# Cosine attention into a highway layer on one Trainium2 core: Newton steps on VectorE for the inverse norms, half of the highway tiles combined in PSUM, and a re-planned order of work

## Chip, core and metric

One core of a Trainium2 chip. The metric is the device time of one execution in microseconds (us), the median of several. Engines are named as in the profile: PE is TensorE's matmul, PEld its weight load, DVE is VectorE, ACT is ScalarE, POOL is GpSimd, SP is SyncE. SP and POOL also issue the DMAs, each in the order of its own instruction stream.

## What is computed

```
q, k, v: [8, 12, 448, 64] float32 (batch, heads, sequence, head size), tau = 0.1
q_n = q / (norm(q) + 1e-6);  k_n = k / (norm(k) + 1e-6)
attn = softmax(q_n @ k_n^T / tau);   y = attn @ v
x = y with heads side by side: [8 * 448 = 3584 tokens, 12 * 64 = 768]
H = max(x @ w_h, 0);  T = sigmoid(x @ w_t + b_t)        w_h, w_t: [768, 768]
out = T * H + (1 - T) * x                                float32
```

## The kernel before

The work is cut two ways. Attention goes by batch (8 batches b), quad (3 per batch: four heads) and pair (two per quad, 48 in all, number n). The highway layer goes by tiles of 128 tokens (28 tiles m: three per batch and, for every second batch, one that gathers the rows left over from two batches).

For each batch the steps are these. POOL issues four loads of q and k into `raw` (L290; six for batch 0), each cast from float32 to float16 on the way. SP issues three loads of v into `vraw` (L311 to L315). VectorE squares q and k (`sq`, L337), folds the squares twice (`f1`, L344; `f2`, L351) and sums them to the squared norms `n2` (`red`, L356). That happens twice per batch, once for each half. Then the inverse norms `rs` are made from `n2`. For batches 0 and 1 this is `newton` (L363 to L373, on VectorE): a shift and a subtraction on the bits for a first guess, then two rounds of three instructions. For batches 2 to 7 it is `power` (L375 to L379): one POOL instruction that raises all 84 norms of each partition to the power -0.5. POOL multiplies q and k by `rs` into `qkn`, six instructions per quad (L411 to L420). SP transposes `qkn` into `qkT` by DMA (L465, two per quad). TensorE multiplies q by k (`sc` and `sl` in PSUM, L508 and L511), ScalarE takes exp into `ex` (L522, L524), TensorE multiplies by v (32 matmuls per pair into a bank of `pb`, L545), and VectorE divides by the row sums: `rd`, `xb`, `st` (L553 to L559).

When the six pairs of a batch are done, SP copies the left-over rows (`sh`, L578) and transposes `xb` into `xT` by DMA (L596). A highway tile is then four matmul groups `ff` (L608, with a bias matmul L611 in the last two), each into one bank of `pb`. The two of w_h are read by VectorE, `d = max(h, 0) - x` (L619). The two of w_t are read by ScalarE, `t = tanh(z / 2)` (L626), into the SBUF tile `t`. Then `g` makes `t = (t + 1) / 2` (L637, VectorE or POOL), `h` makes `d = t * d` (L642, VectorE), `o` makes `o = d + x` (L650, POOL or VectorE), and SP stores `o` (L665).

PSUM has eight banks: four for `sc`, one for `sl` and three for `pb`. The ring of three `pb` banks is shared by the attention product and all four matmul groups of each highway tile.

The order of every engine's instructions is fixed ahead of time by a small planner in Python (class `Planner`). It simulates the engines with a cost in nanoseconds for each step, picks on each free engine the ready step with the lowest number `step` (plus an offset for an engine that is second choice), and writes the instructions out in that order. On the chip each engine runs its stream strictly in that order, so an instruction that waits holds up all behind it. The planner takes 2500 ns for a `power` step. It lets a load be issued while the modelled DMA queue is at most `DEPTH = 2500` ns behind, and lets every DMA land `LATE = 1900` ns after its turn. A step's `takes` and `drops` say which ring slot it takes and frees: `t` frees its `pb` bank when the tanh is done.

Of the kernel before, what the change touches and what calls it, by code (L numbers as in the profile page):

```python
# [44 lines left out]
class Planner:  # L45
# [4 lines left out]
    LATE = 1900  # L50
    DEPTH = 2500
# [112 lines left out]
def kernel(  # L164
# [162 lines left out]
    for b in range(B):  # L327
        parts = [(0, 2), (2, 4), (4, 6)] if b == 0 else [(0, 3), (3, 6)]
        reds = []
        for lo, hi in parts:  # L330
# [68 lines left out]
    for k_ in range(NQUAD):  # L399
# [322 lines left out]
```

## Time and profile before

| | us |
|---|---|
| three executions: lowest, median, highest | 388.15, 389.93, 394.87 |
| the profiled execution, device time | 391.11 |
| its span in the trace | 389.3 |
| busy in it: PE / POOL / DVE / ACT | 270.4 / 261.7 / 206.0 / 184.3 |

The profiled execution is 1.81 us longer than its span, and 1.18 us longer than the median of the three. Busy time is the time in which an engine had an instruction under way. A busy PE may still be slow, because its granted clock varies (1.00 is the upper of its two levels, 2.4 GHz; 0.50 is 1.2 GHz, and a stretch's figure is a mean). The DMA share is the mean over the core's 16 DMA engines of the time in which a packet was under way; packets overlap, so it goes above 1.

### The profile page before, as it was taken

How to read it: one execution, taken by the hardware profiler on the slowest of the kernel's cores; microseconds unless marked ns; L12 is line 12 of the kernel's file. 1: busy time of each engine (PE TensorE's matmuls, PEld its weight loads, DVE VectorE, ACT ScalarE, POOL GpSimd, SP SyncE). 2: the span in 40 equal slices, each digit the busy share in tenths (PEclk: the TensorE clock that was granted, in tenths of full speed). 3: DMA queues.
4: the chain of work that ended last, by engine and by line, in shares of the span. 5: the costliest groups of instructions: out<-in, count | busy, mean ns of one | idle time of the engine just before them, and what ended most of it. 6: DMA issues, size and time to landing. Idle time of an engine off the chain costs nothing.

```text
span 389.3 us, 6889 instructions
## 1 busy us (share of the span) xinstructions
PE 270.4 (69%) x2676; PEld 152.5 (39%) x2676; DVE 206.0 (53%) x403; ACT 184.3 (47%) x268; POOL 261.7 (67%) x225
## 2 busy tenths in 40 slices
PE   0157467991669819399371697836997996898593
PEld 0125233551215505245141364413553654454262
DVE  1899931588415245474385456706784464154133
ACT  1067456682037805537265144801874566366021
POOL 7346773339999996579984998799729992012031
PEclk9998785997569967979886698986998999699698
DMA  7993999999476299995799999944986069311724
GB/s 153 213 191 73 169 181 173 180 222 230 74 133 132 29 168 191 174 211 108 111 146 157 170 192 148 184 61 93 213 158 131 2 121 165 93 42 43 130 50 115
DMA packets 104259, 53.81 MB, mean 138 GB/s; under 512 B 74529, under 2 KB 100641, under 8 KB 104226
## 3 DMA queue, kind: packets, MB, share of 16 engines
q1 hardware_dynamic: 89794, 40.00, 57.3%
q0 software_dynamic: 14432, 13.37, 24.6%
q8 instruction: 21, 0.34, 0.4%
q14 instruction: 12, 0.10, 0.1%
HBM read 39.32 MB, written 11.01 MB: 129 GB/s over the span
## 4 chain that ended last, share of the span: by engine, by line
PE 30%; POOL 29%; DMA 15%; issue 10%; DVE 9%; SPq 4%; ACT 2%; POOLq 1%; DVEq 0%; ACTq 0%
PE pb L608 18%; POOL rs L377 14%; PE pb L545 6%; POOL qkn L420 4%; DMA qkT<-qkn 4%; PE sc L508 4%; DMA raw<-in_k_dram 4%; DMA vraw<-in_v_dram 3%; DMA xT<-xb 3%; POOL qkn L417 2%; POOL qkn L415 2%; DMA out_dram<-o 2%; DVE sq L337 2%; POOL raw L290 2%; POOL t L637 2%
## 5 line engine op out<-in xcount | busy, mean ns | idle before, releaser
L522 ACT ACTIVATE ex<-sc 128x896 f16<-128x896 f32 x144 | 126.1, 924 | 72.1 <-PE sc L508 71.8
L608 PEld LDWEIGHTS <-xT 128*128 128x128 f16 x672 | 68.2, 108 | 123.7 <-issue 52.1
L608 PE MATMUL pb<-w_h,xT 128*128 128x384 f16 x336 | 77.1, 387 | 52.3 <-DMA xT<-xb 42.3
L377 POOL TENSOR_TENSOR rs<-n,half 128x84 f32<-128x84 f32 x6 | 82.8, 13804 | 11.7 <-DVE n L356 9.2
L626 ACT ACTIVATE t<-pb 128x384 f16<-128x384 f32 x56 | 27.6, 493 | 106.1 <-PE pb L611 102.3
L608 PE MATMUL pb<-w_t,xT 128*128 128x384 f16 x336 | 70.4, 350 | 7.1 <-DVE st L559 6.6
L508 PE MATMUL sc<-qkT 64*128 64x448 f16 x288 | 51.8, 392 | 27.5 <-DMA qkT<-qkn 15.9
L545 PE MATMUL pb<-vp,ex 128*128 128x65 f16 x1536 | 62.5, 199 | 5.7 <-DVE d L619 2.0
L650 POOL TENSOR_TENSOR o<-d,xb 128x768 f32<-128x768 f16 x14 | 23.6, 1685 | 61.6 <-DVE d L642 54.7
L545 PEld LDWEIGHTS <-ex 128*128 128x128 f16 x1536 | 58.4, 102 | 16.2 <-issue 10.5
L337 DVE TENSOR_TENSOR sq<-raw 128x2688 f16<-128x2688 f16 (+1 forms) x17 | 30.1, 1771 | 40.1 <-DMA raw<-in_k_dram 40.1
L619 DVE SCALAR_TENSOR_TENSOR d<-pb,xb 128x384 f16<-128x384 f32 x48 | 26.2, 554 | 35.8 <-PE pb L608 35.7
L420 POOL TENSOR_TENSOR qkn<-raw,rs 128x384 f16<-128x384 f16 x45 | 39.9, 902 | 0.1
L637 DVE TENSOR_SCALAR t<-t 128x768 f16<-128x768 f16 x19 | 8.4, 443 | 49.0 <-ACT t L626 49.0
L508 PEld LDWEIGHTS <-qkT 64*128 64x128 f16 x288 | 12.7, 95 | 52.5 <-issue 30.2
L555 DVE TENSOR_TENSOR xb<-pb,rd 128x384 f16<-128x384 f32 x48 | 26.8, 558 | 1.8
L415 POOL TENSOR_TENSOR qkn<-raw,rs 128x448 f16<-128x448 f16 x23 | 22.6, 982 | 7.5 <-DVE rs L372 7.5
L642 DVE TENSOR_TENSOR d<-t,d 128x768 f16<-128x768 f16 x28 | 19.6, 699 | 14.8 <-POOL t L637 14.1
L524 ACT ACTIVATE ex<-sl 128x448 f16<-128x448 f32 x48 | 26.3, 549 | 0.0
L417 POOL TENSOR_TENSOR qkn<-raw,rs 128x384 f16<-128x384 f16 x22 | 24.2, 1098 | 0.0
L553 DVE RECIPROCAL rd<-pb 128x7 f32<-128x7 f32 x48 | 9.6, 199 | 27.4 <-PE pb L545 27.3
L477 POOL TENSOR_TENSOR vp<-vraw,mask 128x768 f16<-128x768 f32 x8 | 12.8, 1599 | 12.2 <-DMA vraw<-in_v_dram 8.6
(56 smaller groups left out, 231.3 us busy)
## 6 DMA issues: line engine op xcount, KB each, us to landing
out_dram<-o SPq DMA_DIRECT2D x48, 192.0 KB, 3.4
vraw<-in_v_dram SPq DMA_DIRECT2D x8, 768.0 KB, 9.7
raw<-in_q_dram POOLq DMA_DIRECT2D x14, 336.0 KB, 7.4
raw<-in_k_dram POOLq DMA_DIRECT2D x14, 336.0 KB, 6.7
vraw<-in_v_dram SPq DMA_DIRECT2D x8, 576.0 KB, 9.0
vraw<-in_v_dram SPq DMA_DIRECT2D x8, 192.0 KB, 8.5
out_dram<-o SPq DMA_DIRECT2D x4, 384.0 KB, 2.5
w_h<-in_moe_w_h_dram POOLq DMA_DIRECT2D x2, 576.0 KB, 9.2
```

What stands on the lines that cost most here:

```text
L337: nc.vector.tensor_mul(sq_r[key][:, 0:n].rearrange("p (t s) d -> p t (s d)", t=2), r, r)
L377: nc.gpsimd.tensor_tensor(out=rs_r[b][:, :, :], in0=n2_r[b][:, :, :], in1=half[:, :].unsqueeze(2).to_broadcast([128, 2, 42]), op=ALU.pow)
L415: eng.tensor_mul(qkn[:, 0:7, 0, :], raw[:, 0, 0], rs[:, 0, 0].unsqueeze(2).to_broadcast([128, 7, D]))
L417: eng.tensor_mul(qkn[:, 1:7, 1, :], raw[:, 0, 1, 0:6], rs[:, 0, 1, 0:6].unsqueeze(2).to_broadcast([128, 6, D]))
L420: eng.tensor_mul(qkn[:, 7:13, g, :].rearrange("p (j i) d -> p i j d", i=2), raw[:, 1, g, 0:6, :].rearrange("p (i j) d -> p i j d", i=2), r ...
L508: nc.tensor.matmul(sc_r[n, j][:, g, 0:S], lhsT=T[:, 448 + 128 * j : 576 + 128 * j], rhs=rhs, start=True, stop=True)
L522: nc.scalar.activation(o, sc_r[n, j][:, :, 0:S], AF.Exp, scale=inv_tau)
L524: nc.scalar.activation(ex[:, 3136 : 3136 + S], sl_r[n][:, 0:S], AF.Exp, scale=inv_tau)
L545: nc.tensor.matmul(u[:, s * 65 : s * 65 + 65], lhsT=l, rhs=r, start=(m == 0), stop=(m == len(ms) - 1))
L555: nc.vector.tensor_tensor(out=xo, in0=u[:, 0:6, 0:D].rearrange("p (g i) e -> p g i e", g=2), in1=rd[:, 0:6].rearrange("p (g i) -> p g i", ...
L608: nc.tensor.matmul(pt[:, 0:MH], lhsT=xT[:, c, :], rhs=w_sb[w][:, c, ms], start=(c == 0), stop=(w == 0 and c == CC - 1))
L626: nc.scalar.activation(t_r[m][:, h], pb_r[m, w, h][:, 0:MH], AF.Tanh, scale=0.5)
```

## The change

Four things are changed. The inverse norms of all eight batches are made by `newton` on VectorE; `power` and its constant `half` are gone. Every second highway tile (odd m, `flat`) is combined in place: tanh writes back into its PSUM bank, VectorE makes `e = (t + 1) * d` in that bank and then `o = 0.5 * e + x` into SBUF, each by halves of 384, and the bank is freed after that. In the other tiles `g` is always on VectorE. The planner treats the SBUF port that VectorE and POOL share as exclusive: a step marked `"port"` doesn't start, in the plan, while one on the other engine holds it. And loads are issued in one order over POOL and SP: a load waits, in the plan, while an earlier-numbered one is ready, and the modelled queue may be 800 ns deep instead of 2500. Several costs are set anew.

```diff
-    LATE = 1900
-    DEPTH = 2500
+    LATE = {"load": 2400, "turn": 2500, "xturn": 1900, "": 1500}
+    DEPTH = 800
...
+            first = min((o.step for q in ready.values() for t, o in q if t <= now and o.dma is not None and o.dma[1] == "load"),
+                        default=0.0)
...
-                    if op.dma is not None and op.dma[1] == "load" and dma_free > now + self.DEPTH:
+                    if op.dma is not None and op.dma[1] == "load" and (dma_free > now + self.DEPTH or op.step > first):
+                        continue
+                    if "port" in op.engs[e] and port_free > now:
                         continue
...
+                if "port" in op.engs[e]:
+                    port_free = now + dur
...
-        def power(b):
-            def fn(op):
-                nc.gpsimd.tensor_tensor(out=rs_r[b][:, :, :], in0=n2_r[b][:, :, :],
-                                        in1=half[:, :].unsqueeze(2).to_broadcast([128, 2, 42]), op=ALU.pow)
-            return fn
...
-            if b < 2:
-                o = add(f"nw{b}_{lo}", ("DVE", 8 * (195 + 14 * (hi - lo) * 1.042)), 6 * b + lo - 4.5, newton(b, lo, hi), **kw)
-            else:
-                o = add(f"nw{b}_{lo}", ("POOL", 2500), 6 * b + lo - 4.5, power(b), **kw)
-                o.deps.append(ini_m)
+            o = add(f"nw{b}_{lo}", ("DVE", 8 * (195 + 14 * (hi - lo) * 1.042), "port"), 6 * b + lo - 4.5, newton(b, lo, hi), **kw)
...
+    FLAT = lambda m: m % 2 == 1
...
-                    def t_fn(op, m=m, w=w, h=h):
-                        nc.scalar.activation(t_r[m][:, h], pb_r[m, w, h][:, 0:MH], AF.Tanh, scale=0.5)
+                    def t_fn(op, m=m, w=w, h=h, flat=flat):
+                        src = pb_r[m, w, h][:, 0:MH]
+                        nc.scalar.activation(src if flat else t_r[m][:, h], src, AF.Tanh, scale=0.5)
...
+        if flat:
+            oo = []
+            for h in range(2):
+                def e_fn(op, m=m, h=h):
+                    t = pb_r[m, 1, h][:, 0:MH]
+                    nc.vector.scalar_tensor_tensor(out=t, in0=t, scalar=1.0, in1=d_r[m][:, h], op0=ALU.add, op1=ALU.mult)
+
+                ee = add(f"e{m}_{h}", ("DVE", 590), s0 + 0.8, e_fn, deps=[el[h], el[2 + h]], drops=[(d_r, m)] if h else [])
+
+                def o_fn(op, m=m, h=h, xsrc=xsrc):
+                    ms = slice(h * MH, h * MH + MH)
+                    nc.vector.scalar_tensor_tensor(out=o_r[m][:, ms], in0=pb_r[m, 1, h][:, 0:MH], scalar=0.5,
+                                                   in1=xsrc()[:, ms], op0=ALU.mult, op1=ALU.add)
+
+                oh = add(f"o{m}_{h}", ("DVE", 590), s0 + 0.8, o_fn, deps=[ee], after=oo, takes=[] if h else [(o_r, m)],
+                         drops=[(pb_r, (m, 1, h))])
```

On POOL, around the inverse norms of batch 2 (`raw2` is its q and k, `vp` the v of the batch before, `o` a highway tile's last step). Before:

```order
L290 DMA raw0_69<-in_q_dram 128x3x448
L477 TENSOR_TENSOR vp0_91<-vraw0_89,mask_67 128x12x64
L290 DMA raw0_69<-in_k_dram 128x3x448
L377 TENSOR_TENSOR rs0_80<-n20_78,half_66 128x84
L411 TENSOR_TENSOR qkn0_83<-raw2_71,rs0_80 128x128
L413 TENSOR_TENSOR qkn0_83<-raw2_71,rs0_80 128x64
L415 TENSOR_TENSOR qkn0_83<-raw2_71,rs0_80 128x7x64
```

Of the change:

```order
L473 TENSOR_TENSOR vp0_90<-vraw0_88,mask_66 128x12x64
L296 DMA raw0_68<-in_q_dram 128x3x448
L296 DMA raw0_68<-in_k_dram 128x3x448
L407 TENSOR_TENSOR qkn0_82<-raw2_70,rs0_79 128x128
L409 TENSOR_TENSOR qkn0_82<-raw2_70,rs0_79 128x64
L411 TENSOR_TENSOR qkn0_82<-raw2_70,rs0_79 128x7x64
```

The instruction of L377 is gone from between the loads and the first multiplication of batch 2 (L411, now L407). The load of v's mask product stands where it stood.

On VectorE, in the same part of the program. Before, batch 2's second half of squares ended in the sum of L356 and nothing followed it there:

```order
L642 TENSOR_TENSOR d1_112<-t1_109,d1_112 128x768
L650 TENSOR_TENSOR o1_115<-d1_112,xb0_98 128x768
L619 SCALAR_TENSOR_TENSOR d2_113<-pb0_120,xb0_98 128x384
L619 SCALAR_TENSOR_TENSOR d2_113<-pb2_122,xb0_98 128x384
L337 TENSOR_TENSOR sq0_72<-raw2_71 128x2688
L344 TENSOR_TENSOR f10_74<-sq0_72 128x1344
L351 TENSOR_TENSOR f20_76<-f10_74 128x672
L356 TENSOR_REDUCE n20_78<-f20_76 128x2x21
L553 RECIPROCAL rd0_96<-pb1_121 128x7
```

Of the change (`e` is L639, its `o` L645, Newton L372 to L378, `red` L362):

```order
L350 TENSOR_TENSOR f10_73<-sq0_71 128x1344
L357 TENSOR_TENSOR f20_75<-f10_73 128x672
L639 SCALAR_TENSOR_TENSOR pb1_120<-pb1_120,d1_111 128x384
L645 SCALAR_TENSOR_TENSOR o1_114<-pb1_120,xb0_97 128x384
L639 SCALAR_TENSOR_TENSOR pb2_121<-pb2_121,d1_111 128x384
L645 SCALAR_TENSOR_TENSOR o1_114<-pb2_121,xb0_97 128x384
L549 RECIPROCAL rd1_96<-pb0_119 128x7
L551 TENSOR_TENSOR xb1_98<-pb0_119,rd1_96 128x2x3x64
L555 TENSOR_TENSOR st1_100<-pb0_119,rd1_96 128x64
L617 SCALAR_TENSOR_TENSOR d2_112<-pb1_120,xb0_97 128x384
L362 TENSOR_REDUCE n20_77<-f20_75 128x2x21
L617 SCALAR_TENSOR_TENSOR d2_112<-pb2_121,xb0_97 128x384
L372 TENSOR_SCALAR rs0_79<-n20_77 128x84
L373 TENSOR_SCALAR rs0_79<-rs0_79 128x84
L376 TENSOR_TENSOR nt0_81<-rs0_79 128x84
L377 SCALAR_TENSOR_TENSOR nt0_81<-nt0_81,n20_77 128x84
L378 SCALAR_TENSOR_TENSOR rs0_79<-nt0_81,rs0_79 128x84
```

Two `e` and two `o` of tile 1, which read and write the banks `pb1` and `pb2`, stand behind the folds of batch 2, and the eight Newton instructions of batch 2 (the last three are left out here) stand behind the sum and behind `d` of tile 2.

On POOL, at the start of the program. Before:

```order
L290 DMA raw0_69<-in_k_dram 128x2x448
L415 TENSOR_TENSOR qkn0_83<-raw0_69,rs0_80 128x7x64
L420 TENSOR_TENSOR qkn0_83<-raw0_69,rs0_80 128x2x3x64
L290 DMA raw1_70<-in_q_dram 128x3x448
L290 DMA raw1_70<-in_k_dram 128x3x448
L290 DMA raw1_70<-in_q_dram 128x3x448
L477 TENSOR_TENSOR vp0_91<-vraw0_89,mask_67 128x12x64
L290 DMA raw1_70<-in_k_dram 128x3x448
L270 DMA w_h_61<-in_moe_w_h_dram 128x3x768 x2
```

Of the change:

```order
L296 DMA raw0_68<-in_k_dram 128x2x448
L296 DMA raw1_69<-in_q_dram 128x3x448
L296 DMA raw1_69<-in_k_dram 128x3x448
L296 DMA raw1_69<-in_q_dram 128x3x448
L296 DMA raw1_69<-in_k_dram 128x3x448
L276 DMA w_h_61<-in_moe_w_h_dram 128x3x768
L473 TENSOR_TENSOR vp0_90<-vraw0_88,mask_66 128x12x64
L276 DMA w_h_61<-in_moe_w_h_dram 128x3x768
L407 TENSOR_TENSOR qkn2_84<-raw0_68,rs0_79 128x128
```

All four loads of batch 1 (`raw1`) and the first of the weights now stand ahead of everything on POOL that waits for data; before, two multiplications of batch 0 and the mask product of v stood between them.

The whole program has 6 `power` instructions fewer and 48 Newton instructions more; POOL has 9 of `g` and 6 of `o` fewer (15 before, 9 now); VectorE has 56 of `e` and its `o` more, 5 of `g`, 14 of `h` and 8 of `o` fewer. ScalarE does 19 of the 24 copies of v (15 before).

## Rows read from the trace of the kernel before

**Rows 1.** The page: busy time, share of the span and instructions of each engine
```profile
PE 270.4 (69%) x2676; PEld 152.5 (39%) x2676; DVE 206.0 (53%) x403; ACT 184.3 (47%) x268; POOL 261.7 (67%) x225
```

**Rows 2.** The page, part 4: shares of the chain that ended last, by engine
```profile
PE 30%; POOL 29%; DMA 15%; issue 10%; DVE 9%; SPq 4%; ACT 2%; POOLq 1%; DVEq 0%; ACTq 0%
```

**Rows 3.** The chain's pieces in order of time: start us, us, what
```profile
89.46 13.77 POOL rs L377
...
247.21 13.74 issue
```

**Rows 4.** Groups by line: busy us, mean ns of one, idle before, releaser
```profile
L377 POOL TENSOR_TENSOR rs<-n,half 128x84 f32<-128x84 f32 x6 | 82.8, 13804 | 11.7 <-DVE n L356 9.2 <-DMA qkT<-qkn 2.6
```

**Rows 5.** GpSimd in order of time, at the fifth of the chain's pieces
```profile
247.14 13.75 POOL L377 TENSOR_TENSOR rs<-n,half 128x84 f32<-128x84 f32 x1 [2.57 <-DMA qkT<-qkn]
```

**Rows 6.** Stretches: us; busy PE, PEld, DVE, ACT, POOL; clock; DMA share; GB/s
```profile
0.00:65.00 65.00, 29.44 (x317) 16.86 (x318) 40.82 (x105) 32.62 (x43) 40.57 (x60) 0.87 0.98 164
65.00:88.00 23.00, 23.00 (x238) 13.25 (x237) 16.16 (x29) 14.53 (x22) 6.82 (x7) 0.94 1.23 201
88.00:266.00 178.00, 114.15 (x1102) 62.90 (x1101) 91.77 (x152) 76.58 (x112) 156.32 (x113) 0.81 0.92 142
266.00:290.00 24.00, 23.80 (x264) 13.59 (x264) 17.09 (x31) 16.09 (x25) 15.22 (x19) 0.93 0.99 188
290.00:358.00 68.00, 60.39 (x644) 34.76 (x644) 29.72 (x68) 40.58 (x61) 36.22 (x25) 0.92 0.42 85
358.00:389.30 31.30, 19.64 (x120) 11.17 (x116) 10.44 (x22) 3.92 (x8) 6.55 (x4) 0.83 0.41 92
```

**Rows 7.** Waits of TensorE: line, releaser, us in total, times, longest
```profile
PE pb L608 <- DMA xT<-xb: 42.3, 7, 10.9
...
PE pb L608 <- DVE st L559: 16.6, 2, 10.0
PE sc L508 <- DMA qkT<-qkn: 15.9, 4, 5.8
...
PE pb L545 <- DVE d L619: 2.0, 1, 2.0
```

**Rows 8.** Waits of SyncE's DMA queue, the same columns
```profile
SPq L465 <- POOL qkn L420: 80.2, 12, 31.4
```

**Rows 9.** Groups by line: one Newton step at two sizes
```profile
L370 DVE TENSOR_TENSOR nt<-rs 128x28 f32<-128x28 f32 x6 | 1.1, 188 | 0.2
...
L370 DVE TENSOR_TENSOR nt<-rs 128x42 f32<-128x42 f32 x4 | 0.8, 202 | 0.1
```

**Rows 10.** VectorE in order of time: start us, us, instruction (batch 1's Newton)
```profile
39.63 0.20 DVE L370 TENSOR_TENSOR nt<-rs 128x42 f32<-128x42 f32 x1
39.87 0.20 DVE L371 SCALAR_TENSOR_TENSOR nt<-nt,n 128x42 f32<-128x42 f32 x1
```

**Rows 11.** Groups by line: the highway's elementwise instructions
```profile
L619 DVE SCALAR_TENSOR_TENSOR d<-pb,xb 128x384 f16<-128x384 f32 x48 | 26.2, 554 | 35.8 <-PE pb L608 35.7
...
L650 POOL TENSOR_TENSOR o<-d,xb 128x768 f32<-128x768 f16 x14 | 23.6, 1685 | 61.6 <-DVE d L642 54.7 <-DVE rd L553 6.9
...
L642 DVE TENSOR_TENSOR d<-t,d 128x768 f16<-128x768 f16 x28 | 19.6, 699 | 14.8 <-POOL t L637 14.1
...
L650 DVE TENSOR_TENSOR o<-d,xb 128x768 f32<-128x768 f16 x10 | 11.7, 1173 | 0.3
...
L637 POOL TENSOR_SCALAR t<-t 128x768 f16<-128x768 f16 x9 | 9.1, 1008 | 13.2 <-ACT t L626 13.2
L637 DVE TENSOR_SCALAR t<-t 128x768 f16<-128x768 f16 x19 | 8.4, 443 | 49.0 <-ACT t L626 49.0
```

**Rows 12.** GpSimd, then VectorE, in order of time
```profile
86.65 1.46 POOL L477 TENSOR_TENSOR vp<-vraw,mask 128x768 f16<-128x768 f32 x1 [3.55 <-PE sl L511]
...
86.71 1.77 DVE L351 TENSOR_TENSOR f<-f 128x672 f16<-128x672 f16 x1
...
91.81 1.55 DVE L337 TENSOR_TENSOR sq<-raw 128x2688 f16<-128x2688 f16 x1
...
94.29 0.51 DVE L351 TENSOR_TENSOR f<-f 128x672 f16<-128x672 f16 x1
```

More of the change, by code (lines that the diff above doesn't have):

```diff
@@ L141, in plan @@
             nxt += [t for t, _, _ in pend if t > now]
+            if port_free > now:
+                nxt.append(port_free)
             if dma_free > now + self.DEPTH:
@@ L344, in f1_fn @@
                     nc.vector.tensor_add(f1_r[key][:, 0:n], s[:, 0:n, 0:32], s[:, 0:n, 32:64])
-            f1 = add(f"f1{b}_{lo}", ("DVE", dve(n * 32, 2)), s0, f1_fn, deps=[sq], takes=[(f1_r, key)], drops=[(sq_r, key)])
+            f1 = add(f"f1{b}_{lo}", ("DVE", dve(n * 32, 2), "port"), s0, f1_fn, deps=[sq], takes=[(f1_r, key)], drops=[(sq_r, key)])
             def f2_fn(op, key=key, n=n):
@@ L426 @@
         for w, n in enumerate((128, 64, 448, 384, 384, 384)):
-            engs = {"POOL": (pool(n), 0.0)}
+            engs = {"POOL": (pool(n), 0.0, "port")}
             if k_ < NPE:
-                engs["DVE"] = (dve(n), 0.0)
+                engs["DVE"] = (dve(n), 0.0, "port")
             o = add(f"nm{k_}_{w}", engs, s0 - 3.5, nm_fn(k_, b, qd, w), deps=[rs_op[b, 2 * qd], rs_op[b, 2 * qd + 1]], after=nms[:1],
@@ L468 @@
                 o = add(f"tr{k_}_{ab}", ("SP", 60), s0 - 2.5, tr_fn, deps=nms, after=[tr[k_, 0]] if ab else [],
-                        takes=[] if ab else [(qkT_r, k_)], drops=[(qkn_r, k_)] if ab else [], dma=(1050, ""))
+                        takes=[] if ab else [(qkT_r, k_)], drops=[(qkn_r, k_)] if ab else [], dma=(1050, "turn"))
                 tr[k_, ab] = o
@@ L477, in vl_fn @@
             nc.gpsimd.tensor_mul(vp_r[b][:, :, 3, 0:D], vraw_r[b][:, :, 3, :], mask[:, :].unsqueeze(2).to_broadcast([128, NH, D]))
-        vlo = add(f"vl{b}", ("POOL", pool(768)), 6 * b - 1.5, vl_fn, deps=vl[b] + [ini_m] + ini_vp, takes=[(vp_r, b)])
+        vlo = add(f"vl{b}", ("POOL", 1500, "port"), 6 * b - 1.5, vl_fn, deps=vl[b] + [ini_m] + ini_vp, takes=[(vp_r, b)])
         prev = vlo
@@ L513 @@
             scr = (sc_r, (n, j)) if j < 3 else (sl_r, n)
-            qk = add(f"qk{n}_{j}", ("PE", 215 if j < 3 else 305), n, qk_fn, deps=qT_op[k_, ab], after=[lastqk], takes=[scr],
+            qk = add(f"qk{n}_{j}", ("PE", 200 if j < 3 else 280), n, qk_fn, deps=qT_op[k_, ab], after=[lastqk], takes=[scr],
                      mode="q", drops=[(qkT_r, k_)] if (ab == 1 and j == 3) else [])
@@ L598 @@
         xt = add(f"xt{m}", ("SP", 60), s0, xt_fn, deps=[xm_ops[b][-1]] if i < 3 else [lefts[b], lefts[b - 1]],
-                 takes=[(xT_r, m)], dma=(900, ""))
+                 takes=[(xT_r, m)], dma=(900, "xturn"))
+        flat = FLAT(m)
         el = []
@@ L624 @@
                 else:
-                    def t_fn(op, m=m, w=w, h=h):
-                        nc.scalar.activation(t_r[m][:, h], pb_r[m, w, h][:, 0:MH], AF.Tanh, scale=0.5)
+                    def t_fn(op, m=m, w=w, h=h, flat=flat):
+                        src = pb_r[m, w, h][:, 0:MH]
+                        nc.scalar.activation(src if flat else t_r[m][:, h], src, AF.Tanh, scale=0.5)
                     o = add(f"t{m}_{h}", ("ACT", 510), s0 - 3, t_fn, deps=[ff],
-                            takes=[(t_r, m)] if h == 0 else [], drops=[(pb_r, (m, w, h))])
+                            takes=[(t_r, m)] if h == 0 and not flat else [],
+                            drops=[] if flat else [(pb_r, (m, w, h))])
                 if h == 1:
```

48 lines of the change are left out of this document (24 added, 24 removed).

## Prediction

> **What bounds the kernel now.** I read the page's busy shares first. No engine is full: TensorE is busy for 69% of the span, POOL for 67%, VectorE for 53% [rows 1]. So the bound is a chain through several engines, and the second view is the chain that ended last. POOL has 29% of it, as much as TensorE [rows 2]. The reader should see that POOL isn't even busiest, but is in the way. The pieces of the chain show why: five of them are one instruction each, L377, of about 13.75 us, the first at 89.46 and the last at 247.21 [rows 3]. The last is labelled "issue", but the timeline shows the same `power` instruction there [rows 5]. All six take 82.8 us of POOL [rows 4]; the sixth is not in the chain. Between `power`'s start and the first multiplication of that batch nothing else of POOL can run.
>
> Third I read the span in stretches [rows 6]. From 88 to 266 us, where five of the six lie, TensorE is busy for 114.15 of 178 us at a granted clock of 0.81. In the three stretches 65 to 88, 266 to 290 and 290 to 358 it is busy for 107.2 of 115 us (93%), at 0.93. That is the pace of this kernel when it isn't held up. Last come TensorE's waits: 42.3 us for `xT`, 16.6 for the last pair of a batch, 15.9 for `qkT` [rows 7]. Two of these are DMAs on SP's queue, which waited 80.2 us in 12 places for `qkn`, POOL's product behind `power` [rows 8]; all that stands behind such a transpose on SP (v loads, `xT`, stores) is late with it.
>
> **The change part by part.** The sums are made against the span of 389.3 us.
>
> *Newton for `power`.* Eight VectorE instructions on 84 elements. One takes 188 ns on 28 and 202 ns on 42 elements [rows 9], 1 ns per element, so 244 ns on 84. Starts lie 0.24 us apart where one lasts 0.20 [rows 10], so 0.28 us each and 2.3 us per batch. That is the lower end. The upper end comes from the port. A fold that started beside POOL's `vp` took 1.77 us, and 0.51 alone, 1.26 us more [rows 12]; if six of the eight (two inputs in SBUF) pay that each, 9.9 us. I take 3, near the lower end, because POOL's next multiplications wait for this very result and mostly don't run beside it. Five times 13.75 less five times 3 is 53.8 us off the chain. Behind Newton, VectorE's stream makes the PSUM reads `rd`, `xb` and `d` 2 to 3 us later, and TensorE's banks with them; the price is in the bank term.
>
> *TensorE's clock.* The 114.15 us were at 0.81 [rows 6]. At 93% busy the same work takes 122.5 us, 55.5 less, which ends at 333.8. At 0.93 it would be 99.9 us of busy time in 107.1, 70.9 less, 318.4. The first agrees with the chain's 53.8. I take half of the difference, 7.7 us, since some gaps of each batch stay (the wait for the last pair isn't POOL's).
>
> *POOL's elementwise work.* Nine `g` at 1.01 us and six `o` at 1.69 us leave POOL [rows 11], 19.2 us. Outside `power`, POOL has 57.9 us of the chain (29% of 389.3, less four pieces of 13.75 labelled POOL) for 178.9 us of work, so I take 0.32 of it: 6.2 us off. Bounds are 0 and 19.2.
>
> *VectorE's share.* Five `g` (0.44), fourteen `h` (0.70) and eight `o` (1.17) leave, 21.4 us; 56 half-tile instructions come. No row shows one that writes float32 into PSUM; the nearest is `d`, which reads PSUM at the same size in 0.554 us, and the upper bound is half a tile's float32 `o` in SBUF, 0.59 [rows 11]. At 0.554 they are 31.0 us, so 9.6 more (11.6 at the upper bound). VectorE has 9% of the chain for 206.0 us of work, 0.17: 1.6 us on. ScalarE's four more copies of v cost nothing while it has 2% of the chain [rows 2].
>
> *The banks.* A flat tile holds two of the three `pb` banks through `e` and `o`, at least 1.1 us longer each, and longer if VectorE comes late: the order shows squares or folds between `d` and `e`. Low end 0, since what hides it is TensorE's other work (q by k has its own banks). High end: behind a square (1.55) and a fold (0.51) [rows 12], with four instructions of 0.554, 4.3 us for each of 14 tiles, 60 us. I take 2. That is near the low end, because today's waits for a bank are small: 2.0 us in one place at L545 [rows 7].
>
> *Loads in one order.* Batch 1's loads and the weights move ahead on POOL, v's loads ahead on SP; 34 loads by POOL and 24 by SP stay. The DMA share is already 0.98 before 65 us [rows 6], so earlier issue can't speed much there. Lower and upper end: one wait of the kind that TensorE has for `qkT` more or less, 5.8 us [rows 7]. I take 0.
>
> *The port in the plan.* It moves rows only. In the first place of rows 12 VectorE's two-input fold waited for POOL. The Trainium skill, page "SBUF — State Buffer", section "SBUF: two separate sides", has the rule: a VectorE instruction with two SBUF inputs and a POOL instruction that reads SBUF take the shared pair one at a time, for the whole instruction. The trace agrees there, but not for `power`: a square at 91.81 and a fold at 94.29 ran under the `power` of 89.46 to 103.23 in 1.55 and 0.51 us, unhindered [rows 3, 12]. By the rule VectorE would be shut out by each `power`, and the 3.0 us from 91.81 to the fold's end would come free five times, 15 us more off, 310 us. By the rows it is 0, and I take 0.
>
> The sum: 389.3 - 53.8 - 7.7 - 6.2 + 1.6 + 2 = 325.2 us of span. The device time is 1.8 above its span, and this execution 1.2 above the median of the three runs, so 326.
>
> **The rivals.**
>
> *TensorE becomes the bound (303).* With the clock whole and all gaps closed, the busy time between 65 and 358 is 23.0 + 99.9 + 23.8 + 60.4 = 207 us, with 65 before and 31.3 after 303 [rows 6]. For it: 65 to 88 ran at 100%. Against it: 290 to 358, with almost no loads left, ran at 89%.
>
> *The DMAs or VectorE take over (353).* Up to 290 us the DMA share sums to 279.5 us. At the highest share of a stretch, 1.23, that fits in 227, and with 99.3 us after it 326.5, just the forecast [rows 6]. At 1.10 it is 254 and 353. VectorE would be busy for 206.0 + 9.6 + 13.6 = 229 us; at 70%, its share from 65 to 88, that is 327, at 63%, its share before 65, 364. For it: both need their best stretch as a mean. Against it: DMA packets that overlap take longer each, so part of the 279.5 is waiting.
>
> *Slower: the flat tiles starve TensorE of banks (408).* If each flat tile stops it for 6 us, because `e` stands behind a whole norm chain and behind reads of pairs that themselves want a bank, 14 times 6 is 84 on top of 324. It cancels the gain from 4.7 us per tile and is slower by over 2% from 5.3. For it: three banks, and a strict order. Against it: today's bank waits.
>
> *The change doesn't do what it says (385).* Newton stands on VectorE behind `d`, which waits for TensorE. If the inverse norms come almost as late as today, 9.9 us for Newton and 3 us of waiting leave 0.85 us per batch of the 13.75.
>
> **How the numbers follow.** Forecast 0.60, with its own range 312 to 342 (below, the other half of the clock's 15.4 and half of what is left of POOL's 19.2; above, Newton at 5 us and one more wait for `qkT`); TensorE-bound 0.15; DMA or VectorE 0.18; banks 0.03; no effect 0.04. 298 to 350 takes in the first two and half of the third, 0.84. By 2% of 389.9 us, which is about what a measurement of this kernel can tell from no change, faster means below 382 and slower above 398. Faster: 0.60 + 0.15 + 0.18 = 0.93. Same: 0.04. Slower: 0.03.
>
> **What would show it.** Right: no L377 and no POOL instruction over 3 us; POOL near 160 us busy; TensorE's 88 to 266 stretch at 90% or more, its waits for `xT` and `qkT` halved; SP's waits for `qkn` well under 80.2. VectorE near 229 us, with `e` and its `o` near 0.55 each. Wrong: waits of L608 or L545 for `e` or `o` (banks); a DMA share held at 1.2 with qkT still late (DMA); POOL's first multiplications waiting long for Newton (order); first q by k later than before (loads).

## The result, and the profile after

The changed kernel takes 356.2 us in the median of four executions (353.6 to 364.7), beside 389.8 before: a ratio of 0.913 (95% interval 0.902 to 0.924). The forecast was 326, with a range of 298 to 350. It has the right sign and is too low by 30 us. The profiled execution has a span of 352.4 us. Some executions of this kernel and its variants ran in a disturbed state some per cent slower; the ratios, and all times of the experiments below, leave them out, and the changed kernel then stands at 354.2 us.

The page of the changed kernel (span; busy time, share and instructions; the DMA share in tenths in 40 slices of the span):

```profile
span 352.4 us, 6950 instructions
...
PE 259.8 (74%) x2676; PEld 147.7 (42%) x2676; DVE 228.2 (65%) x477; ACT 186.8 (53%) x272; POOL 160.3 (45%) x202
...
DMA  7993999969989997993999999996999536403432
```

POOL is busy for 160.3 us and VectorE for 228.2. The forecast said 160 and 229 (from [rows 1]). So the work moved as it was priced. TensorE is busy for 259.8 us with the same instructions, 10.6 less than before, at a mean granted clock of 0.889 (0.855 before).

Stretches of the changed kernel, with the columns of [rows 6]; the bounds follow the work done (the twelfth pair's last matmul ends at 96.0 us, at 89.3 before; that of the last pair at 321.9, at 358.5 before):

```profile
0.00:65.00 65.00, 29.58 (x318) 16.46 (x318) 47.95 (x113) 30.64 (x41) 39.84 (x59) 0.87 1.02 166
65.00:94.00 29.00, 24.65 (x238) 13.79 (x238) 16.54 (x39) 14.57 (x23) 4.99 (x5) 0.88 1.01 189
94.00:286.00 192.00, 152.03 (x1601) 85.90 (x1602) 133.76 (x259) 112.76 (x167) 110.56 (x136) 0.88 0.98 164
286.00:322.00 36.00, 34.32 (x417) 20.73 (x414) 18.18 (x44) 24.92 (x37) 1.64 (x1) 1.00 0.37 86
322.00:352.40 30.40, 19.22 (x104) 10.82 (x104) 11.73 (x24) 3.87 (x8) 3.28 (x2) 0.84 0.39 94
```

The start took 6 us more, the end 1 us less, and the middle, from twelve pairs to 48, 228 us in place of 270. That is 42 us less, where the forecast had about 64. From 94 to 286 us TensorE is busy for 79% at a clock of 0.88; the forecast had 93% at 0.93.

TensorE's waits, with the columns of [rows 7]; L606 is the highway's matmul, L504 q by k, L541 the attention product:

```profile
PE pb L606 <- DMA xT<-xb: 40.0, 8, 8.4
...
PE sc L504 <- DMA qkT<-qkn: 9.9, 3, 5.1
...
PE pb L606 <- DVE d L617: 2.8, 1, 2.8
...
PE pb L541 <- DVE o L645: 0.5, 1, 0.5
```

`qkT` fell from 15.9 to 9.9 us. `xT` hardly moved: 40.0 us, 42.3 before [rows 7]. A bank was waited for 0.5 us behind the flat tiles' `o`, and 2.8 us behind `d`, which isn't new (2.0 at L545 in [rows 7]). The 16.6 us behind `st` are gone. The next rows are the flat tiles' `e` and `o` and one Newton step, by line:

```profile
L639 DVE SCALAR_TENSOR_TENSOR pb<-pb,d 128x384 f32<-128x384 f32 x28 | 15.7, 562 | 10.7 <-ACT pb L625 10.6
...
L645 DVE SCALAR_TENSOR_TENSOR o<-pb,xb 128x384 f32<-128x384 f32 x24 | 13.4, 557 | 0.8
...
L376 DVE TENSOR_TENSOR nt<-rs 128x84 f32<-128x84 f32 x12 | 3.0, 246 | 0.4
```

They are 0.562, 0.557 and 0.246 us, against 0.554 and 0.244 in the forecast.

Then POOL's two longest waits, and SP's for `qkn`:

```profile
POOL o L668 <- DVE d L660: 92.3, 9, 36.8
POOL qkn L407 <- issue: 42.0, 6, 12.3
```

```profile
SPq L461 <- POOL qkn L416: 45.8, 9, 35.4
```

SP's waits for `qkn` fell from 80.2 [rows 8] to 45.8 us. POOL itself waits, 42.0 us in six places, at the first multiplication of a quad (L407). One of these, in order of time (POOL, VectorE, POOL, SP, TensorE; start us, us):

```profile
206.48 0.79 POOL L296 DMA_DIRECT2D raw<-in_k_dram  x1
...
219.96 1.56 DVE L343 TENSOR_TENSOR sq<-raw 128x2688 f16<-128x2688 f16 x1 [2.56 <-DMA raw<-in_k_dram]
...
225.71 0.20 DVE L372 TENSOR_SCALAR rs<-n 128x84 int32<-128x84 int32 x1
...
227.59 0.25 DVE L378 SCALAR_TENSOR_TENSOR rs<-nt,rs 128x84 f32<-128x84 f32 x1
...
227.98 0.39 POOL L407 TENSOR_TENSOR qkn<-raw,rs 128x128 f16<-128x128 f16 x1 [11.93 <-issue]
...
215.32 10.34 SPq L461 DMA_TRANSPOSE qkT<-qkn  x2
...
230.01 3.79 PE L606 MATMUL pb<-w_h,xT 128*128 128x384 f16 x12 [6.59 <-DMA xT<-xb]
...
234.53 1.15 PE L606 MATMUL pb<-w_t,xT 128*128 128x384 f16 x6
```

A load of k is issued at 206.48. VectorE stands idle for 2.56 us until it has landed and squares it at 219.96. The Newton steps end at 227.84, and POOL, which had nothing else to do for 11.93 us, starts the next batch's `qkn` at 227.98. About 4 of these 11.93 us pass until the load has landed; the other 8 are VectorE's work on it and on what stands between. TensorE's wait has another head. Two transposes of an earlier quad took SP until 225.66, 10.34 us where the next two, from 232.51, take 3.21. So the transposes of `xb` weren't issued before 227.12, behind the copies of the left-over rows, and TensorE, whose next instruction is the highway's, waited 6.59 us for `xT` (the last row is the highway's next group).

### The profile page after: what moved, and what is told of

Its sections match the earlier page's. It is cut to its first block, busy times and chain, and to the rows that moved or that the text cites. A ratio compares the mean times of both kernels' runs of the same rounds, so it can differ in the third digit from the quotient of the medians.

```text
span 352.4 us, 6950 instructions
## 1 busy us (share of the span) xinstructions
PE 259.8 (74%) x2676; PEld 147.7 (42%) x2676; DVE 228.2 (65%) x477; ACT 186.8 (53%) x272; POOL 160.3 (45%) x202
## 2 busy tenths in 40 slices
DMA packets 104259, 53.81 MB, mean 153 GB/s; under 512 B 74529, under 2 KB 100641, under 8 KB 104226
## 5 line engine op out<-in xcount | busy, mean ns | idle before, releaser
L606 PEld LDWEIGHTS <-xT 128*128 128x128 f16 x672 | 65.6, 105 | 100.9 <-DMA xT<-xb 42.1
L606 PE MATMUL pb<-w_h,xT 128*128 128x384 f16 x336 | 73.8, 373 | 40.0 <-DMA xT<-xb 40.0
L606 PE MATMUL pb<-w_t,xT 128*128 128x384 f16 x336 | 65.7, 333 | 2.8 <-DVE d L617 2.8
L541 PE MATMUL pb<-vp,ex 128*128 128x65 f16 x1536 | 61.3, 197 | 6.1 <-ACT ex L518 2.8
L504 PE MATMUL sc<-qkT 64*128 64x448 f16 x288 | 51.2, 389 | 19.4 <-DMA qkT<-qkn 9.9
L541 PEld LDWEIGHTS <-ex 128*128 128x128 f16 x1536 | 56.3, 100 | 17.2 <-issue 7.1
L668 POOL TENSOR_TENSOR o<-d,xb 128x768 f32<-128x768 f16 x9 | 14.7, 1638 | 92.3 <-DVE d L660 92.3
L416 POOL TENSOR_TENSOR qkn<-raw,rs 128x384 f16<-128x384 f16 x44 | 41.3, 956 | 0.1
L625 ACT ACTIVATE pb<-pb 128x384 f32<-128x384 f32 x28 | 13.4, 478 | 50.1 <-PE pb L609 49.7
L407 POOL TENSOR_TENSOR qkn<-raw,rs 128x128 f16<-128x128 f16 x22 | 14.3, 648 | 54.5 <-issue 42.0
L343 DVE TENSOR_TENSOR sq<-raw 128x2688 f16<-128x2688 f16 (+1 forms) x17 | 30.7, 1808 | 10.6 <-DMA raw<-in_k_dram 10.6
L504 PEld LDWEIGHTS <-qkT 64*128 64x128 f16 x288 | 12.5, 96 | 44.8 <-issue 29.3
L625 ACT ACTIVATE t<-pb 128x384 f16<-128x384 f32 x28 | 13.8, 493 | 30.6 <-PE pb L609 30.3
L639 DVE SCALAR_TENSOR_TENSOR pb<-pb,d 128x384 f32<-128x384 f32 x28 | 15.7, 562 | 10.7 <-ACT pb L625 10.6
L411 POOL TENSOR_TENSOR qkn<-raw,rs 128x448 f16<-128x448 f16 x22 | 20.5, 934 | 0.0
```

The lines of the kernel that those rows point to most:

```text
L343: nc.vector.tensor_mul(sq_r[key][:, 0:n].rearrange("p (t s) d -> p t (s d)", t=2), r, r)
L411: eng.tensor_mul(qkn[:, 0:7, 0, :], raw[:, 0, 0], rs[:, 0, 0].unsqueeze(2).to_broadcast([128, 7, D]))
L416: eng.tensor_mul(qkn[:, 7:13, g, :].rearrange("p (j i) d -> p i j d", i=2), raw[:, 1, g, 0:6, :].rearrange("p (i j) d -> p i j d", i=2), r ...
L504: nc.tensor.matmul(sc_r[n, j][:, g, 0:S], lhsT=T[:, 448 + 128 * j : 576 + 128 * j], rhs=rhs, start=True, stop=True)
L541: nc.tensor.matmul(u[:, s * 65 : s * 65 + 65], lhsT=l, rhs=r, start=(m == 0), stop=(m == len(ms) - 1))
L606: nc.tensor.matmul(pt[:, 0:MH], lhsT=xT[:, c, :], rhs=w_sb[w][:, c, ms], start=(c == 0), stop=(w == 0 and c == CC - 1))
```

## The experiments

Theory A: what is left are TensorE's waits for `xT` at each batch's end, a latency of their own. Theory B: the new rules put loads too late into the streams of POOL and SP. Theory C: the flat tiles hold the banks. Theory D: the DMA engines set the pace. Times are medians of two to ten executions, or of one where that is said. Ratios are against the kernel before on the same chip; a difference between two kernels is that of their ratios, times 389.8 us, since not all ran on one chip. The runs with altered rules also get another order throughout, since the planner decides anew; the runs with less data keep the order of the kernel that they are made from.

**Newton alone.** The kernel before, with one step exchanged:

```diff
-            if b < 2:
-                o = add(f"nw{b}_{lo}", ("DVE", 8 * (195 + 14 * (hi - lo) * 1.042)), 6 * b + lo - 4.5, newton(b, lo, hi), **kw)
-            else:
-                o = add(f"nw{b}_{lo}", ("POOL", 2500), 6 * b + lo - 4.5, power(b), **kw)
-                o.deps.append(ini_m)
+            o = add(f"nw{b}_{lo}", ("DVE", 8 * (195 + 14 * (hi - lo) * 1.042)), 6 * b + lo - 4.5, newton(b, lo, hi), **kw)
```

> The kernel before with one edit: the inverse norms of batches 2 to 7 by Newton on VectorE, planned at Newton's cost; no flat tiles, no port rule, the old rules for loads. Theory A (what is left are TensorE's waits for xT at the end of each batch, which power never caused, and the other three edits weigh little): 352 to 362 us, xT waits still near 40 us. Theory B (the new rule for loads puts q and k later in POOL's stream and costs time) and theory C (flat tiles hold the banks): 330 to 348, since this kernel has neither.

Measured: 348.4 us, ratio 0.893 (0.885 to 0.901). Newton alone gives more than the whole change. Its page's busy times, with POOL at 188.3 us since all of `g` and `o` may still go there:

```profile
PE 261.8 (75%) x2676; PEld 150.3 (43%) x2676; DVE 226.6 (65%) x446; ACT 186.3 (54%) x271; POOL 188.3 (54%) x221
```

So the three other edits together stand at 7.7 us more, in this one plan. The time is at the edge between the expectations and doesn't decide between A and B by itself. The waits for `xT`, which theory A expected near 40 us, are shorter:

```profile
PE pb L604 <- DMA xT<-xb: 28.4, 6, 11.7
```

Up to 88 us this run is much like the kernel before (twelve pairs end at 89.5 us). The next 178 us, where the kernel before has five `power` instructions, read (columns of [rows 6]):

```profile
88.00:266.00 178.00, 140.04 (x1473) 79.91 (x1471) 136.45 (x238) 100.96 (x149) 128.50 (x147) 0.88 1.02 175
```

TensorE is busy for 79% at a clock of 0.88, in place of 64% at 0.81. That is no more than the changed kernel has from 94 to 286 us, and this run has the old rules for loads.

**The true length of `power` in the plan.** The kernel before, one number:

```diff
-                o = add(f"nw{b}_{lo}", ("POOL", 2500), 6 * b + lo - 4.5, power(b), **kw)
+                o = add(f"nw{b}_{lo}", ("POOL", 13800), 6 * b + lo - 4.5, power(b), **kw)
```

> The kernel before with one number: the planner takes 13800 ns for a power step in place of 2500, so that the rest is laid out around its true length. If power hurt because the plan didn't know its length: 355 to 370 us. If it hurts because POOL can't do its other work meanwhile: 380 to 392.

Measured: 391.2 us, ratio 1.002 (0.999 to 1.005). `power` is as long as ever:

```profile
L377 POOL TENSOR_TENSOR rs<-n,half 128x84 f32<-128x84 f32 x6 | 82.6, 13760 | 4.7 <-DVE n L356 4.7
```

A plan that knows it can't hide it. So the gain comes from taking it off POOL, as the prediction said, and not from a plan that knows its length.

**The old rules for loads.** The changed kernel with:

```diff
-    LATE = {"load": 2400, "turn": 2500, "xturn": 1900, "": 1500}
-    DEPTH = 800
+    LATE = {"load": 1900, "turn": 1900, "xturn": 1900, "": 1900}
+    DEPTH = 2500
...
-                    if op.dma is not None and op.dma[1] == "load" and (dma_free > now + self.DEPTH or op.step > first):
+                    if op.dma is not None and op.dma[1] == "load" and dma_free > now + self.DEPTH:
```

> The changed kernel with the old rules for loads: DEPTH 2500, LATE 1900 for every DMA, and no rule that holds a load behind an earlier-numbered one. Theory B: 335 to 348 us, VectorE's waits for q and k and POOL's for Newton shorter. Theory A: 352 to 362 with xT waits near 40 us. Theory D (the DMA engines are full and set the pace): within 1% of the changed kernel, with the same DMA share.

Measured: 330.3 us, ratio 0.844 (0.839 to 0.849), 27 us less than the changed kernel, and inside the forecast's range. The edit also puts `LATE` back for every DMA, which no run takes apart. This is also a kernel that beats both. Its DMA line, its stretches and its wait for `xT`:

```profile
DMA  6999999959999999999999999797478355114333
```

```profile
0.00:65.00 65.00, 29.07 (x280) 16.39 (x281) 54.27 (x110) 28.48 (x37) 45.06 (x63) 0.85 1.13 191
65.00:94.00 29.00, 25.07 (x268) 14.98 (x268) 25.99 (x51) 15.01 (x24) 18.71 (x22) 0.86 0.98 163
94.00:230.00 136.00, 118.69 (x1309) 69.42 (x1307) 106.61 (x210) 87.05 (x130) 83.72 (x96) 0.95 1.14 202
230.00:265.00 35.00, 32.71 (x359) 18.65 (x356) 20.36 (x52) 26.02 (x39) 16.34 (x21) 1.00 0.60 113
265.00:298.00 33.00, 30.89 (x354) 18.23 (x352) 15.15 (x37) 21.28 (x32) 1.64 (x1) 0.95 0.30 72
298.00:328.70 30.70, 19.42 (x119) 11.06 (x115) 12.30 (x25) 3.87 (x8) 3.27 (x2) 0.89 0.38 93
```

```profile
PE pb L606 <- DMA xT<-xb: 20.5, 6, 6.2
```

The DMA share is 1.13 before 65 us and 1.14 from 94 to 230, where the changed kernel has 1.02 and 0.98; the last load, one of v, is issued at 213 us, in the changed kernel at 270. TensorE is busy for 87% from 94 to 230, at a clock of 0.95. In POOL's stream the last load of k stands behind the products of 14 quads, in the changed kernel's behind 18. The waits for `xT` halve, so about half of them were no latency of their own: theory A is at best half of it.

**The two rules apart.** First without the rule on the order of loads, depth still 800:

```diff
-                    if op.dma is not None and op.dma[1] == "load" and (dma_free > now + self.DEPTH or op.step > first):
+                    if op.dma is not None and op.dma[1] == "load" and dma_free > now + self.DEPTH:
```

> The changed kernel without the rule that holds a load behind an earlier-numbered one; the depth stays 800. On POOL the last load of k then stands behind 16.0 quads' products (changed kernel 18.0, old load rules 14.0). If it is the lateness of the loads in POOL's stream that costs: 338 to 348 us, between the two. If it is the order rule as such: 327 to 334. If it is the depth: 352 to 358.

Measured: 343.1 us, ratio 0.879 (0.876 to 0.882). Then with the depth alone put back:

```diff
-    DEPTH = 800
+    DEPTH = 2500
```

> The changed kernel with the depth back at 2500 and the order rule kept. The last load of k stands behind 13.7 quads' products. Lateness, or the depth: 327 to 335 us. The order rule as such: 350 to 358.

Measured: 342.2 us, ratio 0.877 (0.873 to 0.880). Each gives about half. For the depth both expectations failed, that of 327 to 335 although its last load stood earlier (13.7) than with both rules undone; so the place of the last load alone doesn't give the time.

**A deeper queue still.** The old rules with:

```diff
-    DEPTH = 2500
+    DEPTH = 6000
```

> The old load rules with a depth of 6000 in place of 2500. If earlier is always better: 318 to 327 us. If the gain ended where POOL's other work is displaced: 328 to 340. On POOL the last load of k stands behind 14.5 quads' products (2500: 14.0).

Measured: 332.8 us, ratio 0.855 (0.852 to 0.858), 4 us more than with 2500. By the count of products its last load stands no earlier (14.5 against 14.0), so this doesn't tell what loads that are really earlier would bring.

**Less data, the same order.** The changed kernel, with the loads of v cut from batch 2 on:

```diff
                 vr = vraw_r[b]
+                hh = slice(0, NH if b < 2 else 1)
...
-                    nc.sync.dma_start(vr[64:128, :, :, :].rearrange("p h c d -> p h (c d)"), src[:, :, 3 * D : 7 * D])
+                    nc.sync.dma_start(vr[64:128, hh, :, :].rearrange("p h c d -> p h (c d)"), src[:, hh, 3 * D : 7 * D])
```

(the other two loads of v in the same way)

> The changed kernel in its own order, but from batch 2 on each load of v brings one head in place of twelve, so that about 7.6 of 53.8 MB aren't moved; the output of those batches is computed with old v. Every instruction and issue stays. Theory D (the DMA engines' bandwidth sets the pace): 320 to 340 us. Lateness of q and k in POOL's stream: 348 to 357, hardly changed, since no load is issued earlier.

Measured: 328.7 us, ratio 0.842 (0.837 to 0.847), 28 us less. The expectation from theory B alone, hardly changed, failed. The stretch from 94 us on and the wait for `xT`:

```profile
94.00:260.00 166.00, 148.11 (x1606) 84.92 (x1606) 131.99 (x260) 112.50 (x165) 107.09 (x129) 0.95 0.93 150
```

```profile
PE pb L607 <- DMA xT<-xb: 22.2, 7, 6.9
```

With the same order, TensorE is busy for 89% at 0.95. Now the loads of q and k, which go by POOL's queue, so that SP's instructions stay as they are:

```diff
-        return lambda op: nc.gpsimd.dma_start(raw_r[b][:, t, lo:hi], src[:, 6 * b + lo : 6 * b + hi, :])
+        he = hi if b < 3 else lo + 1
+        return lambda op: nc.gpsimd.dma_start(raw_r[b][:, t, lo:he], src[:, 6 * b + lo : 6 * b + he, :])
```

> The changed kernel in its own order, but from batch 3 on each load of q and k brings one block in place of three (about 4.6 MB of 53.8 less, all in POOL's queue); the output of those batches is computed with old q and k. SP's stream is untouched. If the DMA engines' bandwidth sets the pace: 328 to 340 us. If it was SP's queue behind long loads of v: 350 to 357.

Measured: 331.7 us, ratio 0.851 (0.843 to 0.860), 24 us less.

```profile
94.00:260.00 166.00, 143.02 (x1554) 82.43 (x1555) 125.64 (x250) 107.90 (x159) 97.77 (x127) 0.94 0.90 161
```

So it isn't SP's queue alone behind long loads of v: bytes of either queue count. The pages have 45.16 MB moved with less v and 49.22 with less q and k, beside 53.81, so 8.65 MB (not the 7.6 expected) and 4.6 MB weren't moved. At the 201 GB/s of the best stretch before [rows 6] they would take 43 and 23 us, and 28 and 24 came off.

One way in which bytes hold TensorE up shows in SP's stream. Its 72 transposes take it 130.9 us to issue in the changed kernel, 109.5 with less v and 111.5 with less q and k. In the changed kernel 12 of them take over 2.5 us each, in the other two 4. The 10.34 us above are two of the 12. This isn't what the rules for loads change: with the old ones the 72 take 129.1 us, and again 12 are over 2.5. Last, the cut of v on top of the old load rules:

> The kernel with the old load rules (330.3 us) and, from batch 2 on, one head in place of twelve in each load of v; the output of those batches is computed with old v. If the DMA engines still set the pace once loads are early: 300 to 316 us. If another engine does by then (TensorE's busy share was 78%): 323 to 331.

Measured: 319.0 us, about 9 less than the 330.3 with full loads of v, between the two expectations. The same bytes that cost 28 us where loads are issued late cost about 9 where they are early. A reading that ties theories B and D together, and that no run shows by itself: the late loads leave the DMA engines with time to spare at first and too little afterwards, when the same engines also have to bring `qkT` and `xT`.

**The flat tiles.** The changed kernel with:

```diff
-    FLAT = lambda m: m % 2 == 1
+    FLAT = lambda m: False
```

> The changed kernel with every highway tile combined in SBUF, as before (no tile flat). Theory C (the banks): 335 to 348 us, and fewer waits of L606 and L541 for VectorE. Theory A: 354 to 362, as the changed kernel or a little slower, because h and o come back on VectorE and POOL. Theory B: the same as A.

Measured: 350.8 us, ratio 0.898 (0.892 to 0.904), 5.7 us less than with flat tiles, at the edge of the noise. The same edit on the old load rules:

> The changed kernel with the old load rules and no flat tiles, so Newton and the port rule alone are left of the change. If the flat tiles cost by themselves, as 5 us did on the new load rules: 322 to 327 us. If the load rules are all: 328 to 334. If the flat tiles are worth something once the loads are early: 335 to 345.

Measured: 347.9 us, ratio 0.894 (0.891 to 0.897), 19.6 us more than with flat tiles. Two signs for one edit. And between these two kernels, which have no flat tiles, the rules for loads are worth 1.6 us, inside the noise. TensorE's waits in this last kernel:

```profile
PE pb L606 <- DMA xT<-xb: 22.3, 6, 6.4
...
PE pb L541 <- DVE d L617: 5.6, 1, 5.6
```

Behind `d`, a bank holds TensorE up once, for 5.6 us, and this is the kernel without flat tiles. Behind `st` it waits 8.1 us here and 8.7 with flat tiles. For the flat tiles' own `o` it waits no more than 2.7 us in any run, so theory C has no support.

**The port rule.** The changed kernel with:

```diff
-                    if "port" in op.engs[e] and port_free > now:
+                    if False:
                         continue
```

> The changed kernel with the port rule taken out of the plan (costs left as they are), so that two-input VectorE steps and POOL steps may stand side by side. Theories A to D: 350 to 364 us, no clear difference. If the port rule is what keeps the change from its gain: under 348; if it is worth something: over 365, with squares and folds over 2 us in the mean.

Measured: 358.2 us, ratio 0.918 (0.912 to 0.925). Not told apart from the changed kernel's 0.913 (0.902 to 0.924).

**The left-over rows behind `xT`.** The old load rules with:

```diff
-        sh = add(f"sh{b}", ("SP", 120), 6 * b + 6, sh_fn, deps=[xm_ops[b][-1]], takes=[(xl_r, b // 2)] if b % 2 == 0 else [],
+        sh = add(f"sh{b}", ("SP", 120), 6 * b + 6.9, sh_fn, deps=[xm_ops[b][-1]], takes=[(xl_r, b // 2)] if b % 2 == 0 else [],
```

> The old load rules, with the copy of the left-over rows (two DMAs on SP, about 1.3 us of issue) behind the first transposes of xb in place of ahead of them. Theory A (TensorE's waits for xT at a batch's end are a latency of their own): 318 to 326 us, waits for xT 20.5 to about 12 us. If those waits are covered by what comes later: 328 to 333.

Measured: 324.7 us, ratio 0.834 (0.832 to 0.836).

```profile
PE pb L606 <- DMA xT<-xb: 11.7, 4, 5.1
```

The waits for `xT` fall from 20.5 to 11.7 us and the time lies in the range that theory A gave. But it is only 3.8 us less, of the 8.8: a wait of 8.3 us for `qkT`, which the kernel with the old load rules doesn't have, has come in. And 3.8 us is less than an order moves by itself, as the next runs show.

**How far an order matters by itself.** Three kernels with one number of the planner changed that has to do with neither loads nor tiles:

```diff
-    SYNC = 70
+    SYNC = 85
```

The changed kernel:

> The changed kernel with SYNC 85 in place of 70 in the planner: the same rules, another order. If orders of one rule scatter little: 352 to 360 us. If they scatter by 10 us and more: anywhere from 340 to 370.

Measured: 349.6 us (one execution), about 6 us less than before the shuffle. The old load rules:

> The kernel with the old load rules (330.3 us) with SYNC 85. If the load rules are worth what was measured: 326 to 336 us. If that order was a lucky one: 340 to 350.

Measured: 337.4 us, ratio 0.866 (0.857 to 0.875), 8.7 us more than before the shuffle. And the old load rules without flat tiles:

> The old load rules without flat tiles (347.9 us) with SYNC 85. If the flat tiles are worth 17 us there: 343 to 352 us. If that is scatter: 325 to 340.

Measured: 327.9 us (one execution), about 20 us less than 347.9. So another order under the same rules moves the time by 6 to 20 us, either way. With flat tiles the load rules stand out even so: 354.2 and 349.6 us on one side, 330.3 and 337.4 on the other, 27 us apart with `SYNC` 70 and 12 with 85. Without flat tiles it hangs on the order: 350.8 with the new rules, 347.9 and 327.9 with the old. The flat tiles' 19.6 and -5.7 us are no more than an order moves: what they are worth stays open. So does the split between depth and order of loads, and the 7.7 us between Newton alone and the whole change.

One thing goes with the rule on the order of loads in every plan. TensorE's waits for `xT` and `qkT` together are 46 to 54 us in the five kernels that have this rule and full loads. In the seven that have Newton, full loads and a depth of 2500 or 800 without the rule, they are 20 to 32 us (43 at a depth of 6000). The time doesn't simply follow: without the order rule at a depth of 800 these waits are 25.8 us and the time is 343.1, where the mask product of v alone holds TensorE up for 14.1 us.

## Why the prediction was wrong

*Newton for `power`* was right in kind and in the price of an instruction, and too high in what it frees. L377 is gone, and an instruction of Newton lasts 0.246 us (0.244 forecast). The rival that the change does nothing is out. But Newton alone took 41.6 us off (389.96 to 348.4), against 53.8 and 7.7 for chain and clock together: 20 of the 30 us that the forecast is off. I counted five times 13.75 us as if TensorE had stood still through each `power`. Over these five, the trace of the kernel before has (columns of [rows 6]):

```profile
89.46:103.23 13.77, 3.54 (x12) 1.68 (x13) 11.13 (x18) 0.83 (x2) 13.76 (x1) 0.59 0.97 174
114.89:128.62 13.73, 13.73 (x162) 7.86 (x160) 7.29 (x17) 10.15 (x15) 13.73 (x2) 0.97 0.57 109
168.44:182.18 13.74, 13.74 (x132) 7.64 (x130) 7.40 (x17) 7.79 (x12) 13.74 (x1) 0.93 0.97 199
209.42:223.18 13.76, 6.03 (x24) 2.84 (x25) 5.19 (x10) 0.58 (x2) 13.75 (x1) 0.56 1.19 165
247.14:260.89 13.75, 8.26 (x65) 4.04 (x64) 3.65 (x6) 6.84 (x10) 13.75 (x1) 0.88 0.83 134
```

In the second and third TensorE is busy from end to end; over all five it is idle for 23.5 of 68.8 us. What each `power` made late behind itself isn't in this count, so it doesn't give the 41.6 us. Nor does one plan settle the size: with the port rule and the new costs, but the old load rules and no flat tiles, 41.3 us came off in one order, and 62 in the one execution of a shuffled one. How the 20 us divide between the term and the order of work stays open.

*POOL's and VectorE's shares, and the banks* were right in their sizes: 160.3 and 228.2 us busy, and 0.5 us of new waiting for a bank in place of the 2 taken. The rival of starved banks is out: in no run does TensorE wait more than 2.7 us for the flat tiles' `o`. What POOL's and VectorE's shares of the chain brought (6.2 off, 1.6 on) no run takes apart. All that comes beside Newton and the clock was forecast at 2.6 us off; in the one pair of plans measured it stands at 7.7 on. The rival of TensorE as the bound (303) wasn't reached by any run; the lowest, with most of v not loaded, is 319.0.

*Loads in one order* is one of the two steps that failed. I took 0 with ends of 5.8 us, because the DMA share was already 0.98 before 65 us and the loads of batch 1 moved ahead. I looked at the start of the streams alone. With flat tiles, as the changed kernel has them, the old rules for loads take 12 to 27 us off, two to nearly five times my end. Lateness by itself doesn't explain it. With the old rules the last load of k stands behind the products of 14 quads and is issued at 180 us, in the changed kernel behind 18 and at 247. But in the kernel before it stands behind 19 and comes at 279, and with Newton alone behind 19 and at 232. Through which wait the rules cost their time stays open; the nearest sign is TensorE's longer waiting for `xT` and `qkT` in every plan that has the order rule.

*The pace of 93% at 0.93*, which gave the clock's 7.7 us and bore out the chain's 53.8, is the other step that failed. It failed before any rule for loads was touched: with Newton alone TensorE runs at 79% and 0.88, as in the changed kernel, and the best long stretch of the kernel with the old load rules, from 94 to 230 us, has 87% at 0.95. I carried the share of three good stretches over to the rest, as if POOL had been the only reason for the gaps. One of the three, 290 to 358, holds the sixth `power` itself, from 292.94 to 307.01. And POOL wasn't the only reason: the waits for `xT` stayed at 40.0 of 42.3 us (28.4 with Newton alone). I had laid them to `power` by way of SP's queue, whose waits for `qkn` did fall, without taking those for `xT` along. The clock came to 0.88 and not 0.93 for the same reason. Behind the wait of 6.59 us at 230.01 the granted clock is 0.50, the lower level, from 230 to 232 us, and twelve highway matmuls take 3.79 us, or 0.32 each. From 233.8 us it is 1.00, and six more of the same shape at 234.53 take 1.15, or 0.19 each. The first 2 us behind each of the seven waits for `xT` of 1.7 us and more are at 0.50, so these stops are paid for once more in slow instructions behind them. The chain's 53.8 us and the two TensorE estimates agreed with each other, but all three rest on the assumption that nothing but `power` held the rest up, so their agreement was worth little.

*The second rival came close to the number, and in part by luck.* It said that up to 290 us the DMA share sums to 279.5 us, which gives 326.5 at a share of 1.23 and 353 at 1.10. In the changed kernel the share up to 286 us sums to 284 (65 times 1.02, 29 times 1.01, 192 times 0.98), a mean of 0.99, with 66 us after it: 352. The sum was right. But the share was lower than the rival's 1.10 and the rest shorter than its 99.3 us, and the two offset each other; a share held at 1.2, its sign, didn't come. What the runs bear out is that bytes cost time: in the same order, less v takes 28 us off and less q and k 24. I gave it 0.18, because I took the best stretch's share for what the order would reach. With the old load rules the share is 1.13 and 1.14 in two long stretches, with 0.98 between them, and the time is 330.

*The start* was forecast unchanged and took some 6 us longer (96.0 in place of 89.3 for twelve pairs). With the same rules in a shuffled order twelve pairs take 90.5, so this is no more than an order moves.

## What to carry to other kernels

Time on the chain that ended last isn't time in which the busiest engine stands still: look at what that engine does meanwhile before taking the piece off. When the longest instruction leaves an in-order stream, sum up what the next resource still has to do and ask at what rate it was ever seen to do it over a long stretch, not in its best one. A planner's rule that issues loads just in time is a change to every stream behind it: look at the whole order and its waits, not at the start alone. And where a planner decides the order, shuffle it once by a meaningless number before believing a difference of a few per cent between two of its plans.

## What the runs showed of the hardware that was not expected

VectorE's square of 2688 elements took 5.15 us at 247.00 in the changed kernel (1.55 alone [rows 12]), with POOL's products under way (POOL, then VectorE, start us, us):

```profile
243.02 1.62 POOL L416 TENSOR_TENSOR qkn<-raw,rs 128x384 f16<-128x384 f16 x2
...
247.60 0.41 POOL L407 TENSOR_TENSOR qkn<-raw,rs 128x128 f16<-128x128 f16 x1
247.97 0.30 POOL L409 TENSOR_TENSOR qkn<-raw,rs 128x64 f16<-128x64 f16 x1
248.22 0.94 POOL L411 TENSOR_TENSOR qkn<-raw,rs 128x448 f16<-128x448 f16 x1
249.12 0.82 POOL L413 TENSOR_TENSOR qkn<-raw,rs 128x384 f16<-128x384 f16 x1
249.90 2.93 POOL L416 TENSOR_TENSOR qkn<-raw,rs 128x384 f16<-128x384 f16 x2
...
247.00 5.15 DVE L343 TENSOR_TENSOR sq<-raw 128x2688 f16<-128x2688 f16 x1
```

It was delayed by 3.6 us, longer than any one of POOL's products in that stretch before 249.90. So, by these rows, it wasn't let in between the first few, and the pair of products from 249.90 took 2.93 us in place of the 1.62 of the pair at 243.02, beside which VectorE read PSUM. The Trainium skill, page "SBUF — State Buffer", section "SBUF: two separate sides", has the two taking the shared pair of ports one at a time, each for a whole instruction; the trace agrees that they exclude each other, but the waiter here sat out several instructions, not one. And `power` goes against it, as the prediction's rows showed [rows 12].

POOL's power instruction takes 13.80 us in the mean for 84 elements per partition in the kernel before (13.73 to 14.07), and 13.76 in the plan that knows its length; the eight VectorE instructions that replace it take 2.1 us, from 225.71 to 227.84.
